# Windowed attention with sinks, then an RWKV channel mix: the first loads in one ordered queue, and q and k in rows of two tokens, cast to bf16 by GpSimd before they are transposed

## The chip, the core and the metric

The kernel runs on one core of a Trainium2 chip. The metric is the device time of one execution in microseconds (us), lower is better. Ratios use fast runs alone: runs that lie over 1.5% above the fastest of their kernel are left out of them, though the medians below still count them. The "span" is the profiled execution from its first to its last instruction; it lies 1.7 to 2.1 us below the recorded time of the same run.

## The reference, cut to what matters

Shapes: batch 4, 8 heads, 768 tokens, head size 64; model width 512, hidden width 1024; everything is fp32 in memory.

```python
# attention: each query sees the 4 first keys (sinks) and the 128 keys up to itself
keep = (pos[None, :] < 4) | ((rel >= 0) & (rel < 128))        # rel = query - key
a = softmax(where(keep, q @ k.T / 8, -1e9));  x = a @ v        # heads joined: [4, 768, 512]
# channel mix on x
xk = mu_k * x + (1 - mu_k) * x_prev;  xr = mu_r * x + (1 - mu_r) * x_prev
out = sigmoid(xr @ w_r) * (relu(xk @ w_k) ** 2 @ w_v)
```

## The kernel before

A unit is 256 tokens of one batch, so there are 12 units. Each unit has four steps, one for each pair of heads. TensorE computes scores as [key, query], ScalarE takes their exponential, VectorE multiplies with a 0/1 mask, TensorE multiplies with v (a column of ones beside v gives the sum), and VectorE normalises into `x`. TensorE then transposes `x`, ScalarE copies it to SBUF (`xt`), VectorE makes `xk` and `xr`, and the channel mix of unit u runs as small pieces (`fill()`) between the attention steps of unit u+1. TensorE's program order is fixed by the kernel; the order of the other engines is decided by the scheduler.

Scores need q and k with the head's 64 numbers on partitions, so each is transposed by TensorE. These are the parts that the change touches:

```python
def load(u):                                   # k, q, v of one unit, in rows of one token (256 bytes)
    for dst, src in ((ks, k), (qs, q), (vs, v)):
        for g in range(2):
            s0 = 256 * T + 128 * g
            nc.sync.dma_start(out=dst[:, g, :, :],
                              in_=src[b, :, s0:s0 + 128, :].rearrange("h p d -> p h d"))
...
nc.gpsimd.dma_start(out=wk_sb, in_=moe_w_k...)  # bf16 weights, cast by the transfer; wr, wv later
...
def prepare(u, part):                          # part 0, 1: k; 2, 3: q
    ps = tr_ps.tile([128, NP, 128], FP32, name="tps")
    for c in range(NP):                        # 4 fp32 transposes
        nc.tensor.transpose(out=ps[:, c, :], in_=src[:, g, 2 * c:2 * c + 2, :]..., identity=ident32)
    nc.scalar.copy(out=dst, in_=ps)            # 512 elements per partition, contiguous bf16
...
for n in range(N + 6):                         # u, c = divmod(n, 4)
    ...                                        # sink_scores(u) if c == 0; scores(n); transposes of x
    if n >= 6: fill()                          # a piece of the channel mix
    ...
    if u > 0: prepare(u + 1, c)                # one part of the next unit in every step
```

The softmax here doesn't subtract the row's maximum and nothing guards it: scores larger than these inputs give would overflow.

Of the kernel before, what the change touches and what calls it, by code (L numbers as in the profile page):

```python
# [8 lines left out]
FP32 = mybir.dt.float32  # L9
BF16 = mybir.dt.bfloat16  # L10
AX = mybir.AxisListType
AF = mybir.ActivationFunctionType
ALU = mybir.AluOpType
# [4 lines left out]
def kernel(  # L18
# [14 lines left out]
    nc = tc.nc  # L33
    B, H, S, D = q.shape
    Dm = H * D
    Dff = moe_w_k.shape[1]
    assert (B, H, S, D) == (4, 8, 768, 64) and int(window) == 128 and int(n_sink) == 4
    NS = 4
    NT = S // 256
    NP = H // 2  # L40
    NC = Dm // 128
    NF = Dff // 128
    U = B * NT
    scale = 1.0 / (D ** 0.5)

    const = ctx.enter_context(tc.tile_pool(name="const", bufs=1))
    ld = ctx.enter_context(tc.tile_pool(name="ld", bufs=3))
    kt_pool = ctx.enter_context(tc.tile_pool(name="kt", bufs=3))
# [5 lines left out]
    tr_ps = ctx.enter_context(tc.tile_pool(name="tr_ps", bufs=2, space=PSUM))  # L54
# [3 lines left out]

    raw = {}

    def load(u):
        b, T = divmod(u, NT)
        ks = ld.tile([128, 2, H, D], FP32, name="ks")
        qs = ld.tile([128, 2, H, D], FP32, name="qs")
        vs = ld.tile([128, 2, H, D], FP32, name="vs")
        for dst, src in ((ks, k), (qs, q), (vs, v)):
            for g in range(2):
                s0 = 256 * T + 128 * g
                nc.sync.dma_start(out=dst[:, g, :, :],  # L69
                                  in_=src[b, :, s0:s0 + 128, :].rearrange("h p d -> p h d"))  # L70
        raw[u] = (ks, qs, vs)

    load(0)
    load(1)


    ident32 = const.tile([128, 128], FP32, name="ident32")
    make_identity(nc, ident32)
    ident = const.tile([128, 128], BF16, name="ident")
    nc.gpsimd.tensor_copy(out=ident, in_=ident32)  # L80


    mask = const.tile([128, 2, 2, 2, 128], BF16, name="mask")
    mask0 = const.tile([128, 2, 3, 128], BF16, name="mask0")

    def keep(ap, kind):
        if kind == "U":
            nc.gpsimd.affine_select(out=ap, in_=ap, compare_op=ALU.is_ge, fill=0.0, base=-1,
                                    pattern=[[0, 2], [-1, 128]], channel_multiplier=1)
        else:  # L90
            nc.gpsimd.affine_select(out=ap, in_=ap, compare_op=ALU.is_ge, fill=0.0, base=0,
                                    pattern=[[0, 2], [1, 128]], channel_multiplier=-1)

    nc.gpsimd.memset(mask0, 1.0)
    keep(mask0[:, :, 0, :], "D")
    keep(mask0[:, :, 1, :], "U")
    keep(mask0[:, :, 2, :], "D")
    nc.gpsimd.memset(mask0[0:NS, :, 0:2, :], 1.0)

    wk_sb = const.tile([128, NC, Dff], BF16, name="wk_sb")  # L100
    wv_sb = const.tile([128, NF, Dm], BF16, name="wv_sb")
    wr_sb = const.tile([128, NC, Dm], BF16, name="wr_sb")
    wv_h = const.tile([128, NF, Dm], BF16, name="wv_h")
    nc.gpsimd.dma_start(out=wk_sb, in_=moe_w_k.rearrange("(c p) f -> p c f", p=128))
    mu_k_sb = const.tile([128, NC], FP32, name="mu_k_sb")
    nc.scalar.dma_start(out=mu_k_sb, in_=moe_mu_k.rearrange("(c p) -> p c", p=128))
    mu_r_sb = const.tile([128, NC], FP32, name="mu_r_sb")
# [7 lines left out]
    v_bufs = [const.tile([128, 2, H, D + 1], BF16, name=f"v{i}") for i in range(3)]  # L115
# [7 lines left out]
    ksink = [const.tile([128, NP * 136], BF16, name=f"ksink{i}") for i in range(2)]  # L123
# [9 lines left out]
    for t in vsink:  # L133
# [1 line left out]

    spread = const.tile([128, 128], BF16, name="spread")
    nc.gpsimd.memset(spread, 0.0)
    nc.gpsimd.tensor_copy(out=spread[0:NS, 0:4 * H].rearrange("p (h s) -> p h s", s=NS),
                          in_=ident[0:NS, 0:NS].unsqueeze(1).to_broadcast([NS, H, NS]))


    kts, qts = {}, {}

    def prepare(u, part):
        b, T = divmod(u, NT)
        ks, qs, vs = raw[u]
        g = part % 2
        if part == 0:
            kts[u] = kt_pool.tile([128, 2, NP, 128], BF16, name="kt")
            qts[u] = kt_pool.tile([128, NP, 256], BF16, name="qt")  # L150
        src, dst = ((ks, kts[u][:, g, :, :]), (qs, qts[u][:, :, 128 * g:128 * g + 128]))[part // 2]
        ps = tr_ps.tile([128, NP, 128], FP32, name="tps")
        for c in range(NP):
            nc.tensor.transpose(out=ps[:, c, :],  # L154
                                in_=src[:, g, 2 * c:2 * c + 2, :].rearrange("p a d -> p (a d)"),
                                identity=ident32)
        nc.scalar.copy(out=dst, in_=ps)  # L157
        if part < 2:
            nc.gpsimd.tensor_copy(out=v_bufs[u % 3][:, g, :, 0:D], in_=vs[:, g, :, :])  # L159
        if part == 3 and T == 0:  # L160
            kz = ksink[b % 2].rearrange("p (c w) -> p c w", w=136)
            for a in range(2):
                rows = slice(64 * a, 64 * a + 64)
                nc.gpsimd.tensor_copy(out=kz[rows, :, 4 * a:4 * a + NS],
                                      in_=kts[u][rows, 0, :, 0:NS])

    def sink_values(b):
        ps = tr_ps.tile([128, H, D], FP32, name="tps")
# [8 lines left out]
    def sink_scores(u):  # L177
        b, T = divmod(u, NT)
        ps = tr_ps.tile([128, 256], FP32, name="tps")
        for c in range(NP):  # L180
            nc.tensor.matmul(out=ps, lhsT=ksink[b % 2][:, 128 * c:128 * c + 128],  # L181
                             rhs=qts[u][:, c, :], start=(c == 0), stop=(c == NP - 1))
        es[u] = e_pool.tile([128, 256], BF16, name="es")
        nc.scalar.activation(out=es[u], in_=ps, func=AF.Exp, scale=scale)
# [19 lines left out]
    def masked(n):  # L204
        e = live[n]
        if (n // NP) % NT > 0:
            nc.vector.tensor_tensor(out=e, in0=e, in1=mask.rearrange("p a g k q -> p a (g k q)"),  # L207
                                    op=ALU.mult)
        else:
            nc.vector.tensor_tensor(out=e[:, :, 128:], in0=e[:, :, 128:],  # L210
                                    in1=mask0.rearrange("p a k q -> p a (k q)"), op=ALU.mult)
# [34 lines left out]
    def transposed(u, half):  # L246

        b, T = divmod(u, NT)
        x, xt = xs[u], xts[b % 2]
        c0 = 2 * half  # L250
        ps = tr_ps.tile([128, 2, 256], BF16, name="tps")
        for i in range(2):
            for g in range(2):
                nc.tensor.transpose(out=ps[:, i, 128 * g:128 * g + 128],  # L254
                                    in_=x[:, g, 128 * (c0 + i):128 * (c0 + i) + 128],
                                    identity=ident)
        t0 = 2 + 256 * T
        nc.scalar.copy(out=xt[:, c0:c0 + 2, t0:t0 + 256], in_=ps)
# [68 lines left out]
    N = U * NP  # L327

    def fill(count=1):
        for _ in range(count):  # L330
            next(chunks, None)

    ORDERED = {mybir.EngineType.PE}
    with tc.manual_schedule(engines=ORDERED):
        for part in range(4):
            prepare(0, part)
        for n in range(N + 6):
            u, c = divmod(n, NP)
            inner = n < N
            if inner:  # L340
                if c == 0 and u % NT > 0:
                    sink_scores(u)
                scores(n)
            if c % 2 == 1 and 2 <= n < N + 2:
                transposed((n - 2) // NP, ((n - 2) % NP) // 2)
            if n >= 6:
                fill()
            if inner:
                masked(n)
            if 1 <= n < N + 1:  # L350
                values(n - 1)
            if c % 2 == 1 and 2 <= n < N + 2:
                mix((n - 2) // NP, ((n - 2) % NP) // 2, 0)
            if n >= 6:
                fill()
            if inner and u + 1 < U:
                if u == 0 and c == 3:
                    for part in range(4):
                        prepare(1, part)
                elif u > 0:  # L360
                    prepare(u + 1, c)
                if c == 3 and u + 2 < U:
                    load(u + 2)
            if c % 2 == 0 and 3 <= n < N + 3:
                mix((n - 3) // NP, ((n - 3) % NP) // 2, 1)
            if c == 2 and inner and u % NT == 0:
                sink_values(u // NT)
            if c % 2 and n >= 6:
                fill()
            if n == 0:  # L370
                nc.gpsimd.dma_start(out=wr_sb, in_=moe_w_r.rearrange("(c p) f -> p c f", p=128))
                nc.gpsimd.dma_start(out=wv_sb, in_=moe_w_v.rearrange("(c p) f -> p c f", p=128))
            if n == 5:

                for f in range(NF):
                    nc.vector.tensor_scalar(out=wv_h[:, f, :], in0=wv_sb[:, f, :], scalar1=0.5,
                                            scalar2=None, op0=ALU.mult)
        for _ in chunks:
            pass

# [34 lines left out]
```

## Time and profile before

| | before |
|---|---|
| median | 206.14 us (4 runs, 204.73 to 208.56; 205.99 without the slow one) |
| span, mean granted TensorE clock | 203.1 us, 0.95 |
| busy: TensorE, VectorE, ScalarE, GpSimd | 178.5, 135.1, 125.3, 32.0 us |
| chain that ended last, by engine | PE 67%, DVE 11%, SPq 9%, DMA 7%, ACT 4% |
| unit 0's channel mix ends | 52.06 us |
| mean period of the next nine units | 14.15 us |

The last two rows are what the argument uses most. They are read from the instructions that write the kernel's output tile (`o_sb`, two per unit): the start of a unit's second one is taken as the end of that unit (in unit 0 that instruction itself takes 0.67 to 0.69 us in every run). The first number is the cost of the start. The difference between two units is the price of one unit once the pipeline is full. Units 0 and 9, whose distance divided by nine is the period:

```profile
52.06 0.68 DVE L315 SCALAR_TENSOR_TENSOR o_sb<-th,mm 128x512 f32<-128x512 f32 x1
179.40 0.68 DVE L315 SCALAR_TENSOR_TENSOR o_sb<-th,mm 128x512 f32<-128x512 f32 x1
```

### The profile page before, as it was taken

The numbers are of one execution on the slowest core, as the hardware profiler recorded it, in microseconds if no ns is written. First come the engines' busy times: TensorE is split into PE (matmuls) and PEld (weight loads), VectorE is DVE, ScalarE is ACT, GpSimd is POOL, SyncE is SP. The second block draws the span as 40 slices with busy tenths as digits, with TensorE's granted clock in tenths as the row PEclk, the third lists the DMA queues.
The fourth block names the chain that finished last, engine by engine and source line by source line (L and its number), as shares of the span: only waits on it lengthen the run. The fifth ranks groups of instructions, "written<-read, shape, count | busy, mean of one in ns | idle before, by whom it ended". The sixth has DMA issues, their size and how long they took to land.

```text
span 203.1 us, 4308 instructions
## 1 busy us (share of the span) xinstructions
PE 178.5 (88%) x1668; PEld 120.8 (59%) x1668; DVE 135.1 (66%) x348; ACT 125.3 (62%) x201; POOL 32.0 (16%) x68
## 2 busy tenths in 40 slices
PE   1717706899999999999999999999999999999992
PEld 1405505576765766856756767658567577566650
DVE  0026306975886977868869858868879498698731
ACT  2434604685785766876776857957767758656340
POOL 8935011313112020030030020030300000000000
PEclk9975755899999999999999999999999999999999
DMA  7999999998895995987879627402011020020202
GB/s 124 211 229 197 193 214 224 194 224 161 213 227 134 254 210 131 242 186 175 206 174 245 154 54 207 98 26 90 0 55 52 0 97 11 3 103 0 106 0 103
DMA packets 81508, 28.07 MB, mean 138 GB/s; under 512 B 76368, under 2 KB 77904, under 8 KB 81488
## 3 DMA queue, kind: packets, MB, share of 16 engines
q1 hardware_dynamic: 78336, 25.17, 57.3%
q0 software_dynamic: 2096, 2.62, 7.5%
q8 instruction: 13, 0.21, 0.4%
q10 hardware_dynamic: 1056, 0.00, 0.3%
q14 instruction: 7, 0.06, 0.1%
HBM read 24.12 MB, written 6.29 MB: 150 GB/s over the span
## 4 chain that ended last, share of the span: by engine, by line
PE 67%; DVE 11%; SPq 9%; DMA 7%; ACT 4%; issue 2%; DVEq 0%
PE mm L290 17%; PE mm L310 15%; PE mm L302 11%; SPq L69 9%; PE tps L154 7%; DMA ks<-in_k_dram 7%; PE sc L197 5%; PE o L234 4%; PE tps L254 3%; DVE o_sb L315 3%; DVE xk L277 2%; PE o L223 2%; PE tps L181 2%; ACT e L201 2%; DVE xr L277 2%
## 5 line engine op out<-in xcount | busy, mean ns | idle before, releaser
L201 ACT ACTIVATE e<-sc 128x1024 bf16<-128x1024 f32 (+1 forms) x48 | 45.9, 957 | 14.5 <-PE sc L197 12.7
L290 PE MATMUL mm<-xk,wk_sb 128*128 128x256 bf16 x384 | 50.0, 273 | 0.6 <-DVE xk L277 0.4
L310 PE MATMUL mm<-wv_h,kk 128*128 128x512 bf16 x192 | 48.3, 379 | 0.0
L207 DVE TENSOR_TENSOR e<-e,mask 128x1024 bf16<-128x1024 bf16 x32 | 22.0, 689 | 25.6 <-ACT e L201 25.5
L294 ACT ACTIVATE rl<-mm 128x512 bf16<-128x512 f32 x48 | 29.0, 603 | 15.9 <-PE mm L290 14.7
L290 PEld LDWEIGHTS <-wk_sb 128*128 128x128 bf16 x384 | 34.7, 98 | 6.2 <-issue 1.8
L159 POOL CAST v<-vs 128x512 bf16<-128x512 f32 x24 | 18.1, 767 | 112.6 <-PE o L234 53.7
L157 ACT CAST kt<-tps 128x512 bf16<-128x512 f32 x24 | 14.1, 586 | 32.0 <-PE tps L154 32.0
L154 PE MATMUL tps<-ident,ks 128*128 128x128 f32 x96 | 17.1, 311 | 12.2 <-DMA ks<-in_k_dram 12.2
L234 PE MATMUL o<-v,e 128*128 128x65 bf16 x352 | 21.3, 197 | 4.5 <-POOL v L159 4.2
L310 PEld LDWEIGHTS <-kk 128*128 128x128 bf16 x192 | 16.9, 98 | 13.1
L302 PE MATMUL mm<-wr_sb,xr 128*128 128x512 bf16 x96 | 24.4, 380 | 0.0
L234 PEld LDWEIGHTS <-e 128*128 128x128 bf16 x352 | 18.2, 100 | 8.7 <-issue 3.9
L154 PEld LDWEIGHTS tps<-ident,ks 128*128 128x128 f32 x96 | 13.5, 161 | 16.1 <-issue 7.4
L277 DVE SCALAR_TENSOR_TENSOR xr<-td,mu_r_sb,xt 128x256 bf16<-128x256 bf16 x48 | 21.7, 483 | 0.0
L295 DVE TENSOR_TENSOR kk<-rl 128x512 bf16<-128x512 bf16 x48 | 20.1, 420 | 1.9 <-ACT rl L294 1.6
L277 DVE SCALAR_TENSOR_TENSOR xk<-td,mu_k_sb,xt 128x256 bf16<-128x256 bf16 x48 | 21.2, 477 | 0.0
L210 DVE TENSOR_TENSOR e<-e,mask 128x768 bf16<-128x768 bf16 x16 | 8.9, 554 | 18.3 <-ACT e L201 17.8
L239 DVE TENSOR_TENSOR x<-o,rec 128x256 bf16<-128x256 f32 x48 | 20.1, 418 | 0.7
L197 PE MATMUL sc<-qt,kt 64*128 64x128 bf16 (+1 forms) x256 | 18.8, 248 | 1.6 <-ACT e L201 0.9
L315 DVE SCALAR_TENSOR_TENSOR o_sb<-th,mm 128x512 f32<-128x512 f32 x24 | 16.3, 679 | 3.5 <-PE mm L310 3.5
L197 PEld LDWEIGHTS <-kt 64*128 64x128 bf16 x256 | 8.9, 95 | 15.2 <-issue 14.6
(46 smaller groups left out, 168.7 us busy)
## 6 DMA issues: line engine op xcount, KB each, us to landing
ks<-in_k_dram SPq DMA_DIRECT2D x24, 256.0 KB, 4.7
qs<-in_q_dram SPq DMA_DIRECT2D x24, 256.0 KB, 4.8
vs<-in_v_dram SPq DMA_DIRECT2D x24, 256.0 KB, 5.2
out_dram<-o_sb SPq DMA_DIRECT2D x24, 256.0 KB, 2.1
wk_sb<-in_moe_w_k_dram POOLq DMA_DIRECT2D x1, 1024.0 KB, 9.5
wv_sb<-in_moe_w_v_dram POOLq DMA_DIRECT2D x1, 1024.0 KB, 12.9
wr_sb<-in_moe_w_r_dram POOLq DMA_DIRECT2D x1, 512.0 KB, 6.9
mu_k_sb<-in_moe_mu_k_dram ACTq DMA_DIRECT2D x1, 2.0 KB, 3.7
```

What stands on the lines that cost most here:

```text
L154: nc.tensor.transpose(out=ps[:, c, :], in_=src[:, g, 2 * c:2 * c + 2, :].rearrange("p a d -> p (a d)"), identity=ident32)
L197: nc.tensor.matmul(out=sc[:, a, o0:o1], lhsT=lhs[rows], rhs=qt[rows, c, q0:q0 + o1 - o0], start=True, stop=True)
L201: nc.scalar.activation(out=e[:, :, lo:], in_=sc[:, :, lo:], func=AF.Exp, scale=scale)
L207: nc.vector.tensor_tensor(out=e, in0=e, in1=mask.rearrange("p a g k q -> p a (g k q)"), op=ALU.mult)
L234: nc.tensor.matmul(out=o[:, g, a, :], lhsT=e[:, a, e0:e0 + 128], rhs=rhs, start=(T == 0 and i == 0), stop=(i == len(blocks) - 1), skip_gro ...
L239: nc.vector.tensor_tensor(out=xs[u][:, :, 128 * c:128 * c + 128].rearrange("p g (a d) -> p g a d", a=2), in0=o[:, :, :, 0:D], in1=rec.to_b ...
L277: nc.vector.scalar_tensor_tensor(out=dst[:, c0 + i, :], in0=td[:, i, :], scalar=mu[:, c0 + i:c0 + i + 1], in1=prv[:, i, :], op0=ALU.mult, ...
L290: nc.tensor.matmul(out=ps[:, i, :], lhsT=wk_sb[:, c, 128 * f:128 * f + 128], rhs=xk[:, c, :], start=(c == 0), stop=(c == NC - 1), skip_gro ...
L294: nc.scalar.activation(out=rl, in_=ps, func=AF.Relu)
L302: nc.tensor.matmul(out=ps, lhsT=xr[:, c, 128 * g:128 * g + 128], rhs=wr_sb[:, c, :], start=(c == 0), stop=(c == NC - 1))
L310: nc.tensor.matmul(out=ps, lhsT=kk[:, f, 128 * g:128 * g + 128], rhs=wv_h[:, f, :], start=(f == 0), stop=(f == NF - 1))
L315: nc.vector.scalar_tensor_tensor(out=o_sb, in0=th[g], scalar=1.0, in1=ps, op0=ALU.add, op1=ALU.mult)
```

## The change

It has four intents. All first loads go through one queue in a fixed order. q and k come in rows of two tokens (512 bytes), so partition p holds tokens 2p and 2p+1. GpSimd casts them to bf16, laid out as pairs of heads, so that their transposes are bf16 and one PSUM tile holds all of k, or q, of a unit. The pieces of the second unit's preparation move, so that channel-mix work stands ahead of the third unit's transposes. Masks, sinks and v's loads follow the new order of keys, and the weights arrive in fp32 and are cast on the engines.

```diff
-            nc.sync.dma_start(out=dst[:, g, :, :], in_=src[...].rearrange("h p d -> p h d"))
+            nc.sync.dma_start(out=t[:, hs, :, :].rearrange("p h j d -> p h (j d)"),
+                in_=src[b, hs, ...].rearrange("h (p j) d -> p h (j d)", j=2))     # k, q
 ...
+    with tc.manual_schedule(engines={SP}):
+        load(0); wk32; load(1, "kq"); wr32; load(1, "v"); wv32; load(2)           # one queue, in this order
 ...
+    def cast(u):                     # GpSimd: 2 casts each of k and q, then the 2 of v
+        halves[u, name] = kt_pool.tile([128, NP, 2, 2, D], BF16, name=name + "b")
+        nc.gpsimd.tensor_copy(out=halves[u, name][:, :, j, :, :], in_=raw[u, name][:, :, j, :]...)
 ...
-        ps = tr_ps.tile([128, NP, 128], FP32, name="tps")     # 4 fp32 transposes, 4 times a unit
+        ps = tr_ps.tile([128, NP, 2, 128], BF16, name="tps")  # 8 bf16 transposes, twice a unit
-        nc.scalar.copy(out=dst, in_=ps)
+        nc.scalar.copy(out=qts[u].rearrange("p c (t j) -> p c j t", j=2), in_=ps)
 ...
+    keep(): every mask selection in two halves of 64 partitions
+    weights_k(): 4 VectorE casts of wk, at step 2;  weights_rv(): GpSimd casts wr,
+                 VectorE scales wv to wv_h in 4 pieces, at step 4
 ...
-                elif u > 0: prepare(u + 1, c)
+                if c == 0: cast(u + 1)
+                elif c >= 2: prepare(u + 1, c - 2)            # k at step 2, q at step 3
```

## The prediction

> **What bounds the kernel now.** I read the page's table of engines and its strip of slices first, then the chain that ended last in order of time, then the timelines of single engines over the first 40 us.
>
> ```profile
> PE 178.5 (88%) x1668; PEld 120.8 (59%) x1668; DVE 135.1 (66%) x348; ACT 125.3 (62%) x201; POOL 32.0 (16%) x68
> PE   1717706899999999999999999999999999999992
> PEclk9975755899999999999999999999999999999999
> DMA  7999999998895995987879627402011020020202
> ```
>
> One digit is 5.08 us. TensorE is the bound from about slice 8 to slice 39, with two holes before that, and the DMA engines are full through exactly those early slices. The busy time of stretches says the same: in 40 to 180 us PE is busy 139.2 of 140 us. So there are two stages: a start that waits, and some 163 us in which only less TensorE work helps. The chain shows where one gives way to the other:
>
> ```profile
> 18.64 13.47 DMA ks<-in_k_dram
> 32.11 0.14 issue
> 32.25 1.09 PE tps L154 x4
> ```
>
> The columns are start, length, what. The k rows of the third unit (a unit is 256 tokens of one batch) were issued at 18.6 and landed at 32.1. The PE timeline shows what TensorE had reached by then:
>
> ```profile
> 4.41 1.09 PE L154 MATMUL tps<-ident,ks 128*128 128x128 f32 x4 [4.41 <-DMA ks<-in_k_dram]
> 14.82 0.27 PE L234 MATMUL o<-v,e 128*128 128x65 bf16 x2 [3.21 <-POOL v L159]
> 24.59 0.36 PE L234 MATMUL o<-v,e 128*128 128x65 bf16 x6
> 32.25 1.09 PE L154 MATMUL tps<-ident,ks 128*128 128x128 f32 x4 [7.29 <-DMA ks<-in_k_dram]
> ```
>
> TensorE takes its instructions in program order. Unit 0's attention is nearly done, unit 1 is prepared, but the transposes of unit 2 stand in the queue ahead of every channel-mix matmul, so 7.29 us pass idle. At 32.25 no channel mix has run at all. What is left then takes 203.1 - 32.25 = 170.85 us. That includes about 4 us of tail.
>
> What a transpose costs in the saturated stage comes from the chain and from one group:
>
> ```profile
> 39.59 0.44 PE tps L154 x4
> 187.60 0.22 PE tps L254 x4
> L154 PE MATMUL tps<-ident,ks 128*128 128x128 f32 x96 | 17.1, 311 | 12.2 <-DMA ks<-in_k_dram 12.2
> ```
>
> Four fp32 transposes of q/k hold PE's queue 0.44 us (110 ns each). Four bf16 transposes of x of the same shape hold it 0.22 us here; in the timeline at 97.78 the next matmul starts 0.25 us later (55 to 63 ns each). The 311 ns in the group are latency of pipelined instructions and not what one costs.
>
> **What the Trainium skill says, and whether this trace agrees.** "DMA: Bandwidth & Descriptors", Specifications, puts the smallest transfer at line rate at 512 bytes, and its section "Why small descriptors are slow (HBM only)" gives a 256-byte descriptor 8 beats plus about 3 cycles of overhead. The trace has the 256-byte side only: in 2.5 to 4.5 us, before the weights flow, 214 GB/s, which is 16 x 256 B / 214 GB/s = 19 ns per packet and engine. Nothing here shows 512 bytes. "TensorE: Matmul & The Clock Gate", Back-to-back issue gap, has 55.6 ns for 128 columns once warm; the 0.22 us for four agree. "ScalarE: Activation LUTs", What ACT_TABLE_LOAD costs, has 186 ns + 0.833 ns per element, so 613 ns for 512; here the copies of kt take 586 and the 1024-wide exponential 1029. "SBUF — State Buffer", SBUF: two separate sides, says GpSimd and VectorE lock each other out of a shared port pair for whole instructions. The trace fits: a GpSimd cast of v takes 0.61 us while VectorE is idle (14.15) and 0.82 at 39.10, beside which a pair of xr operations took 1.23 us where others took 0.87.
>
> **The change part by part.**
>
> *Transposes.* A unit still has 16 transposes, now bf16: 16 x 0.060 = 0.96 us for 16 x 0.110 = 1.76 us, 0.80 us saved. Units 0 and 1 are in the start, so 10 units count: 8.0 us, all on the path.
>
> *Copies out of PSUM on ScalarE.* Four of 512 (4 x 0.586 = 2.34 us per unit) become two of 1024. At 586 + 512 x 0.833 = 1013 ns each (an estimate with the skill's slope) that is 2.03. ScalarE's time is not the bound, but its latency enters: q's copy is followed at the next unit's head by the sink scores, with one channel-mix piece of 0.87 us in between. Today 0.586 us fits under 0.87; 1.01 us plus some 0.1 to 0.2 us of handover, sometimes behind a 0.6 us Relu, does not. I give this 0.2 to 0.3 us per unit, 2.5 us in all. Net of steady state: 8.0 - 2.5 = 5.5 us.
>
> *GpSimd.* It now casts k and q as well: 4 more casts of 512 elements per unit, 4 x 0.77 = 3.1 us on top of 1.5, or 4.6 in a unit of about 15 us. It keeps up. VectorE loses perhaps 0.2 us per cast by the port, 0.8 us on 11.5 us of work per unit. Still under PE.
>
> *GpSimd at the start.* This is a loss. Setup ended at 10.6 us before, and k and q did not need it; now their casts stand behind it in GpSimd's order. The build's order shows seven mask selections split in two (+7 x 0.36 = 2.5 us), one more memset (+0.47), one more small copy (+0.16), the weight issue gone (-0.88), the identity's cast gone (-0.24): setup ends near 12.6. Then two k casts with the rest of the setup between them, q's two casts done at about 16.0, v's at 17.2. Transposes of q take till 17.0, their copy till 18.1. First scores at 18.1 instead of 10.0. Before, the values then waited for v till 14.8, so 4 to 5 us are really lost.
>
> *The order of the first loads.* One queue carries k0, q0, v0, the channel mix's first matrix, k1, q1, second matrix, v1, third matrix, k2. Before k2 is complete that is 2.62 MB in 512-byte rows, 1.05 MB in 256-byte rows and 5.24 MB of fp32 weights. At 16 engines: 320 packets of 512 B at 20 to 31 ns = 6.4 to 10 us; 256 of 256 B at 19.5 = 5.0; weights at an estimated 26 GB/s per engine, 12.6 us. With a start near 3.0 (k's first 256 KB were in use at 4.4), k2 lands at 27 to 31 us, its cast ends by 32.5. So it comes 1 to 4 us earlier at most.
>
> *Pieces moved forward.* This is what I count on at the start. PE no longer meets unit 2's transposes until after four channel-mix pieces, three more score groups and two more value groups. The chain of unit 0 sets the pace: scores at 18.1, and at the present distance of 1.65 us (16.36 to 18.03) the fourth at about 22.7; exponential, mask, values, normalising and its transposes end at about 26.3; 16 transposes of unit 1 on a cold clock to 28.0; copy to 29.1; sink scores and scores to 30.2. From there TensorE has work without a gap. Between 30.2 and unit 2's transposes lie 4 x 0.87 + 3 x 0.33 + 2 x 0.36 = 5.2 us or more, so k2 is wanted at about 35 and is there.
>
> *The sum.* At 30.2 the changed kernel stands about where the old one was at 32.25: it has still unit 0's last x transposes behind it (-0.3 us of remaining work), and has done the scores that the old one had done too. So 2.0 us gained at the start, 5.5 in steady state, and 1.0 us taken off for VectorE's in-order queue, which casts the first matrix ahead of its first mask and scales the third one as soon as the queue reaches it, landed or not. Span: 203.1 - 2.0 - 5.5 + 1.0 = 196.6 us. The recorded median of 205.99 lies 2.9 above that span; the same shift gives 199.5, which I round to 199.3.
>
> **The rivals.**
>
> First, the start is lost to GpSimd. For it: GpSimd's setup is serial, 10 us long already, and everything now passes through it. Against: TensorE had 7.3 us of idle time to give away before 32.25. If GpSimd's casts run at 0.8 us and each step slips, saturation starts at 34 instead of 30.2, and the time is about 203, within 2%.
>
> Second, loads become the bound. Weights now cross as fp32 on the same queue, ahead of k2, and v in 64-partition pieces. For it: DMA is at 90% in all early slices and moves 200 GB/s whatever is asked. If the mean stayed at 205 GB/s, 8.9 MB would need 43 us; k2 would come 8 us after it is wanted: 207, the same or slower. Against: the old kernel read the same weights and 3.4 MB of rows within 30 us, about 290 GB/s of reads, and 2 to 4 KB rows have little overhead.
>
> Third, ScalarE's longer copy and the port eat the whole steady gain: 0.8 us per unit of new waiting, about 204.5. The copies' slack above makes 0.3 more likely.
>
> Fourth, better than I say: 512-byte rows as fast per packet as 256, no waits at unit heads, masks early: 8 + 5 us, about 193.
>
> **Range and chances.** The steady saving is the surest term (4 to 8 us); the start can go from -3 to +5. Adding them, 194.0 to 204.5 should hold it 8 times in 10. The 2% line is at 201.9, some 2.6 us above my figure. Faster 0.70, within 2% 0.26, slower 0.04.
>
> **What would show it.** Right: q/k transposes in the chain at 0.22 to 0.25 us per four, PE's q/k transpose work about halved; first scores near 18 us; the first channel-mix matmul near 30 us or earlier and ahead of unit 2's transposes; no wait of several us on k's loads there; POOL busy about 70 us. A wait of the sink scores on the qt copy, 0.2 to 0.3 us, about ten times. Wrong: a gap of some us before unit 2's transposes with a DMA or the k cast as releaser (the second rival); PE idle above 5 us after 40 us; masks late on VectorE because of the weight casts; PE's first saturated slice later than today's seventh or eighth.

## The result, and the profile after

The changed kernel takes 218.23 us (median of 4 runs, 216.8 to 218.66) against 206.14 us. The ratio is 1.060, with a 95% interval of 1.052 to 1.068: slower. Ratios are the mean time of one kernel's fast runs over that of the other's fast runs of the same rounds, so not quite the ratio of the medians quoted.

| | before | after |
|---|---|---|
| span, mean granted clock | 203.1, 0.95 | 216.9, 0.98 |
| busy PE, DVE, ACT, POOL | 178.5, 135.1, 125.3, 32.0 | 170.8, 152.7, 126.3, 70.9 |
| chain by engine | PE 67%, DVE 11%, ACT 4% | PE 40%, DVE 28%, ACT 16%, POOL 9% |
| unit 0 ends | 52.06 | 60.27 |
| mean period of nine units | 14.15 | 14.75 |
| last two periods | 11.21, 8.58 | 11.21, 8.58 |

The 13.8 us of span split cleanly: 8.2 at the start (60.27 - 52.06), 5.4 in the steady state (9 x 0.60), 0.2 in the tail. Units 0 and 9 after:

```profile
60.27 0.68 DVE L359 SCALAR_TENSOR_TENSOR o_sb<-th,mm 128x512 f32<-128x512 f32 x1
193.01 0.68 DVE L359 SCALAR_TENSOR_TENSOR o_sb<-th,mm 128x512 f32<-128x512 f32 x1
```

TensorE's work did fall, and both stages got longer. The page's engines and strip after, 5.42 us per digit:

```profile
PE 170.8 (79%) x1646; PEld 110.3 (51%) x1668; DVE 152.7 (70%) x348; ACT 126.3 (58%) x177; POOL 70.9 (33%) x130
PE   0004467947998788999989889989898899899992
PEclk9999999976999999999999999999999999999999
DMA  6999999900159299488496792791102011020102
```

The DMA engines now stand nearly idle in slices 8 and 9, so loads are not the bound. TensorE begins late, dips at slice 8 (43 to 49 us), has a granted clock of 0.7 and 0.6 there and in the next slice, and then stands mostly at 8 and 9 where before it stood at 9.

The chain that ended last (start, length, what) says who set the pace of the start:

```profile
17.52 1.07 POOL qb L175 x2
...
24.24 2.03 DVE e L254
...
33.84 1.21 ACT qt L200
...
41.13 2.82 DVE wv_h L386 x4
43.95 1.49 DVE kk L339 x2
```

Before, this part of the chain was one wait for a load of k. Now it runs through GpSimd's casts, then VectorE's mask, then ScalarE's copy of q, then VectorE's scaling of a weight. TensorE's timeline shows the same as its waits (start, length, then in brackets the idle time before and what ended it):

```profile
20.97 0.51 PE L241 MATMUL sc<-qt,kt 64*128 64x256 bf16 x4 [1.39 <-ACT qt L200]
26.31 0.51 PE L278 MATMUL o<-v,e 128*128 128x65 bf16 x6 [2.04 <-DVE e L254]
46.84 0.39 PE L298 MATMUL tps<-ident,x 128*128 128x128 bf16 x2 [2.88 <-DVE x L283]
```

First scores came at 20.97 (10.03 before), the first channel-mix matmul at 36.57 (36.45 before). VectorE's timeline, and two GpSimd lines beside it, give the reason for the second and third wait:

```profile
15.35 6.50 DVE L380 CAST wk_sb<-wk 128x1024 bf16<-128x1024 f32 x4 [15.35 <-DMA wk<-in_moe_w_k_dram]
24.15 2.10 DVE L254 TENSOR_TENSOR e<-e,mask 128x768 bf16<-128x768 bf16 x1
41.05 2.90 DVE L386 TENSOR_SCALAR wv_h<-wv 128x1024 bf16<-128x1024 f32 x4
```

```profile
14.52 0.61 POOL L175 CAST kb<-ks 128x512 bf16<-128x512 f32 x1
23.95 1.90 POOL L383 CAST wr_sb<-wr 128x2048 bf16<-128x2048 f32 x1
```

Unit 0's first k cast starts only at 14.52, behind GpSimd's setup. The mask multiplication that takes 0.56 us elsewhere (28.57) took 2.10 us: it started 0.20 us after GpSimd's cast of wr and ended 0.40 us after it, as if it had stood still until the cast was done. The weight casts took 1.6 us each while GpSimd cast q, k and v beside them.

In the steady state, TensorE's waits between 60 and 178 us are, before and after:

```profile
PE tps L254 <- ACT qt L157: 0.7, 3, 0.2
```

```profile
PE tps L225 <- ACT qt L200: 3.0, 5, 0.7
PE sc L241 <- ACT qt L200: 2.1, 3, 0.7
PE tps L298 <- ACT kt L191: 2.0, 3, 0.7
PE tps L298 <- DVE x L283: 1.7, 3, 1.0
PE mm L334 <- DVE xk L321: 0.7, 2, 0.5
```

(total us, times, longest.) Some eight units lie in that stretch, so 9.5 us are 1.2 us per unit where 0.1 were. Of these 5.1 are waits at a unit's head for ScalarE's copy of q. The groups by shape show the two new copies (busy, mean ns, idle before):

```profile
L200 ACT COPY qt<-tps 128x1024 bf16<-128x1024 bf16 x12 | 15.9, 1322 | 1.1 <-PE tps L197 1.1
L191 ACT COPY kt<-tps 128x1024 bf16<-128x1024 bf16 x12 | 12.1, 1009 | 14.8 <-PE tps L188 14.8
```

Same element count, but q's copy, which writes every second element, takes 1322 ns. What the change was for did happen. Eight bf16 transposes hold the queue 0.54 us (start to start), where two groups of four fp32 ones held it 0.88 us:

```profile
92.45 0.61 PE L188 MATMUL tps<-ident,kb 128*128 128x128 bf16 x8
92.99 0.40 PE L241 MATMUL sc<-qt,kt 64*128 64x256 bf16 x6
```

### The profile page after: what moved, and what is told of

The parts are those of the page before. It is cut to its first block, busy times and chain, and to the rows that moved or that the text cites. A ratio compares the mean times of both kernels' runs of the same rounds, so it can differ in the third digit from the quotient of the medians.

```text
span 216.9 us, 4338 instructions
## 1 busy us (share of the span) xinstructions
PE 170.8 (79%) x1646; PEld 110.3 (51%) x1668; DVE 152.7 (70%) x348; ACT 126.3 (58%) x177; POOL 70.9 (33%) x130
## 4 chain that ended last, share of the span: by engine, by line
PE 40%; DVE 28%; ACT 16%; POOL 9%; issue 6%; POOLq 0%; ACTq 0%; DVEq 0%
PE mm L334 12%; PE mm L354 9%; PE mm L346 6%; ACT qt L200 5%; DVE xk L321 5%; DVE o_sb L359 4%; ACT e L245 4%; PE sc L241 4%; ACT rl L338 3%; PE o L278 3%; DVE xr L321 3%; DVE e L254 3%; DVE kk L339 3%; DVE e L251 3%; DVE x L283 3%
## 5 line engine op out<-in xcount | busy, mean ns | idle before, releaser
L334 PE MATMUL mm<-xk,wk_sb 128*128 128x256 bf16 x384 | 51.8, 276 | 1.3 <-DVE xk L321 0.7
L354 PE MATMUL mm<-wv_h,kk 128*128 128x512 bf16 x182 | 45.3, 379 | 0.5
L251 DVE TENSOR_TENSOR e<-e,mask 128x1024 bf16<-128x1024 bf16 x32 | 23.4, 731 | 29.9 <-ACT e L245 29.9
L175 POOL CAST kb<-ks 128x512 bf16<-128x512 f32 x24 | 17.1, 739 | 28.1 <-DMA ks<-in_k_dram 27.9
L321 DVE SCALAR_TENSOR_TENSOR xr<-td,mu_r_sb,xt 128x256 bf16<-128x256 bf16 x48 | 24.9, 538 | 0.0
L339 DVE TENSOR_TENSOR kk<-rl 128x512 bf16<-128x512 bf16 x48 | 21.9, 458 | 2.3 <-ACT rl L338 2.3
L321 DVE SCALAR_TENSOR_TENSOR xk<-td,mu_k_sb,xt 128x256 bf16<-128x256 bf16 x48 | 22.0, 489 | 0.0
L175 POOL CAST qb<-qs 128x512 bf16<-128x512 f32 x24 | 17.1, 743 | 14.3 <-DMA qs<-in_q_dram 13.3
L188 PE MATMUL tps<-ident,kb 128*128 128x128 bf16 x96 | 8.4, 234 | 16.5 <-POOL kb L175 16.5
L191 ACT COPY kt<-tps 128x1024 bf16<-128x1024 bf16 x12 | 12.1, 1009 | 14.8 <-PE tps L188 14.8
```

The source lines that it names most:

```text
L175: nc.gpsimd.tensor_copy(out=halves[u, name][:, :, j, :, :], in_=raw[u, name][:, :, j, :].rearrange("p (c a) d -> p c a d", a=2))
L251: nc.vector.tensor_tensor(out=e, in0=e, in1=mask.rearrange("p a g k q -> p a (g k q)"), op=ALU.mult)
L321: nc.vector.scalar_tensor_tensor(out=dst[:, c0 + i, :], in0=td[:, i, :], scalar=mu[:, c0 + i:c0 + i + 1], in1=prv[:, i, :], op0=ALU.mult, ...
L334: nc.tensor.matmul(out=ps[:, i, :], lhsT=wk_sb[:, c, 128 * f:128 * f + 128], rhs=xk[:, c, :], start=(c == 0), stop=(c == NC - 1), skip_gro ...
L339: nc.vector.tensor_tensor(out=kk[:, 2 * f2:2 * f2 + 2, :], in0=rl, in1=rl, op=ALU.mult)
L354: nc.tensor.matmul(out=ps, lhsT=kk[:, f, 128 * g:128 * g + 128], rhs=wv_h[:, f, :], start=(f == 0), stop=(f == NF - 1))
```

## The experiments

Twelve kernels ran; all were correct within the reference's tolerance. "Unit 0 ends" and "period" (mean of nine) are read as above.

| run | built on | median us | ratio to before (95%) | unit 0 ends | period |
|---|---|---|---|---|---|
| before | | 205.0 to 206.1 | 1 | 52.06 | 14.15 |
| after | | 218.23 | 1.060 (1.052 to 1.068) | 60.27 | 14.75 |
| e1_q_early | after | 211.58 | 1.028 (1.024 to 1.032) | 55.43 | 14.41 |
| e2_no_casts | after | 211.20 | 1.028 (1.025 to 1.032) | 56.94 | 14.33 |
| e3_masks_first | after | 213.32 | 1.040 (1.035 to 1.045) | 57.62 | 14.45 |
| e4_casts_first | after | 212.86 | 1.037 (1.033 to 1.042) | 55.15 | 14.64 |
| e5_q_early_no_casts | after | 205.14 | 1.000 (0.996 to 1.005) | 54.17 | 13.93 |
| e6_order_only | before | 205.79 | 1.003 (0.999 to 1.007) | 53.61 | 14.12 |
| e7_start | after | 207.17 | 1.009 (1.005 to 1.014) | 49.28 | 14.72 |
| e8_start_q_early | e7 | 207.10 | 1.007 (0.999 to 1.014) | 50.92 | 14.63 |
| e9_dma_cast | e7 | 200.93 | 0.978 (0.973 to 0.982) | 49.23 | 14.05 |
| e10_act_k | e7 | 203.12 | 0.992 (0.985 to 0.998) | 48.77 | 14.25 |
| e11_flat_copy | after | 224.67 | 1.096 (1.091 to 1.100) | 61.06 | 15.27 |
| e12_q_natural | e9 | 198.77 | 0.969 (0.965 to 0.972) | 48.45 | 13.80 |

The theory: the start is lost to serial work on GpSimd and VectorE, and the steady state to two separate things, the latency of q's copy at the unit's head and VectorE slowed by GpSimd's casts. Rivals: the loads and the new order of pieces; TensorE or ScalarE itself.

### e1_q_early: the transposes of k and q one step earlier

```diff
-                elif c >= 2: prepare(u + 1, c - 2)
+                elif c <= 2: prepare(u + 1, c - 1)          # k at step 1, q at step 2
```

> Edit: the k and q transposes of the next unit move one step earlier (steps 1 and 2 of a unit instead of 2 and 3), so that the qt copy (1.32 us) has a whole step to land before the sink scores. Theory A (in steady state TensorE loses its time at unit heads, waiting for that copy; the changed kernel has 6.4 us of sink scores waiting for qt and 3.5 us of scores waiting for qt, 7 us of it after 50 us): these waits vanish, the period of a unit falls from 14.75 us to about 14.1, time about 212 us. Theory B (VectorE, slowed by GpSimd's casts, sets the pace): the waits move to the xk and x operands and the time stays above 216.5 us.

The period fell from 14.75 to 14.41. The waits of a unit's head on q's copy are gone from the stretch 60 to 178 us (5.1 us after the change). In exchange the wait of x's transposes on `x` rose to 6.1 us there (1.7), and 2.8 us of the same transposes wait behind q's copy:

```profile
PE tps L298 <- DVE x L283: 6.1, 5, 2.2
PE tps L298 <- ACT qt L200: 2.8, 3, 0.9
```

So the latency of the copy at the head was real, and worth 0.34 us per unit, about half of what was expected. Moving it exposes VectorE. Unit 0 ended 4.8 us earlier too, although the first channel-mix matmul stood at 36.61 as before it: the idle time behind the scaling of wv was 2.15 us instead of 2.88, and the strip of the granted clock has no digit below 9.

### e2_no_casts: from unit 2 on, GpSimd casts neither k nor q

This kernel is wrong: units 2 and up use the q and k of units 0 and 1. It passes the tolerance only because the scores of these inputs are tiny.

```diff
         for name in "kq":
+            if u >= 2:
+                halves[u, name] = halves[u % 2, name]; continue
```

> Wrong result on purpose: from unit 2 on the k and q casts on GpSimd are left out and the transposes read the casts of units 0 and 1 again; everything else stays. Theory B (port contention of the casts with VectorE): xr falls from 538 to about 485 ns, the 768-wide mask from 718 to about 555, VectorE's busy time from 152.7 to about 143 us, the period from 14.75 to about 14.2 us and the time to about 212 us. Theory A (the qt copy's latency): the waits on qt stay near 8 us and the time stays within 2 us of the changed kernel's (above 216).

The period fell to 14.33, although the waits on q's copy stayed (3.1 + 2.1 us in the same stretch). Where the gain came from is seen in VectorE's groups between 70 and 160 us, first of the changed kernel, then of this one:

```profile
L321 DVE SCALAR_TENSOR_TENSOR xr<-td,mu_r_sb,xt 128x256 bf16<-128x256 bf16 x25 | 13.8, 569 | 0.0
L251 DVE TENSOR_TENSOR e<-e,mask 128x1024 bf16<-128x1024 bf16 x16 | 12.1, 756 | 14.4 <-ACT e L245 14.4
```

```profile
L324 DVE SCALAR_TENSOR_TENSOR xr<-td,mu_r_sb,xt 128x256 bf16<-128x256 bf16 x26 | 11.8, 472 | 0.0
L254 DVE TENSOR_TENSOR e<-e,mask 128x1024 bf16<-128x1024 bf16 x16 | 11.0, 689 | 16.2 <-ACT e L248 16.2
```

Without the casts the same operations are back at the durations of the kernel before (477 and 690 ns in this stretch). GpSimd's casts cost VectorE 97 ns on each xr and 67 on each mask, and the kernel 0.42 us per unit. Here too the idle time behind the scaling of wv was shorter (1.30 us) and the clock did not fall afterwards, and unit 0 ended 3.3 us earlier. What the low clock of the changed kernel cost can be read off: the same TensorE work, from the end of this wait to the start of the next, took 5.31 us there (46.84 to 52.15) and 2.81 us here (45.97 to 48.78), so 2.5 us. The lines that bound these stretches (46.84 is shown above), first of the changed kernel, then of this one:

```profile
53.53 0.60 PE L225 MATMUL tps<-qt,ksink 128*128 128x256 bf16 x4 [1.38 <-ACT qt L200]
```

```profile
45.97 0.29 PE L301 MATMUL tps<-ident,x 128*128 128x128 bf16 x2 [1.30 <-DVE x L286]
50.21 0.60 PE L228 MATMUL tps<-qt,ksink 128*128 128x256 bf16 x4 [1.43 <-ACT qt L203]
```

### e3_masks_first and e4_casts_first: the start, one engine at a time

e3 makes VectorE issue the first masks in program order, with the weight casts behind them. e4 makes GpSimd cast unit 0's q, k and v right after the small mask, ahead of the rest of its setup.

```diff
 e3: +        head.enter_context(tc.manual_schedule(engines={DVE}))       # until step 3
     -            if n == 2: weights_k()
     +            if n == 3: weights_k(); head.close()
 e4: +    setup.enter_context(tc.manual_schedule(engines={Pool}))
      memset(...small mask...)
     +    cast_qk(0, "k"); ones of v_bufs; cast_qk(0, "q"); cast_v(0)     # was: after all of the setup
```

> Edit: VectorE issues unit 0's masks and normalisations before the four casts of the first matrix, which stood first in its queue (6.5 us from 15.35, so that the first mask ran only at 22.43). If these casts hold the start up: unit 0's values come about 2 us earlier, the first channel-mix matmul at about 34.5 instead of 36.6 us, time about 216 us. If GpSimd's chain (casts behind setup) sets the start alone: first mask at 22.4 as before, no change (218). The casts may also land on the path further on, ahead of the last normalisation of unit 0: then 218 to 220.

> Edit: GpSimd's order at the start is fixed: identity, first mask, then unit 0's casts of k, q and v, then the rest of the setup. If the casts' place behind the setup is what delays the start: the first scores come at about 12 us instead of 21, the first channel-mix matmul at about 30 instead of 36.6, time 212 to 214 us, with a wait before unit 2's transposes for k2 (landed at about 32.5). If the loads set the start: first channel-mix matmul after 35 us and time above 217. VectorE's first mask behind the first matrix's casts (15.4 to 21.9) could eat most of the gain: then first values at about 22.5 and time about 217.

Each gained only part: unit 0 ended at 57.62 and 55.15 instead of 60.27. In e4 the first scores came at 11.10, ten us earlier, and yet the first channel-mix matmul came at 36.42 where it was 36.57. TensorE waited 5.14 us for GpSimd's sink setup, now pushed back, and 4.18 us for an `x` whose VectorE was casting weights. In e3 the first channel-mix matmul came even later (38.20), and TensorE waited 3.73 us for `x` behind the weight casts. The theory that these casts hold up the first mask was a miss: in the changed kernel they end at 21.85 and the first exponential only at 22.32. The wait of 3.73 us cannot be compared with the one that comes before the low clock in the changed kernel. It lies before TensorE has reached full pace: eight channel-mix matmuls of e3 take 1.89 us at first and 1.04 from 40.93 on.

```profile
38.20 1.89 PE L334 MATMUL mm<-xk,wk_sb 128*128 128x256 bf16 x8
40.93 1.04 PE L334 MATMUL mm<-xk,wk_sb 128*128 128x256 bf16 x8
```

(The strip of the clock shows 9 in those first slices too, so there neither it nor the mean clock says anything about the pace.) After full pace was reached, the profiles of variants of the change show a fall in e11 (behind a wait of 2.89 us) and twice in e8 (waits of 2.63 and 2.21 us), and none in e1 behind 2.15 us. No run tells what length of idleness brings it. VectorE's and GpSimd's lines of e3 settle what slows a VectorE operation:

```profile
22.86 1.82 DVE L254 TENSOR_TENSOR e<-e,mask 128x768 bf16<-128x768 bf16 x1 [0.65 <-ACT e L245]
29.82 2.49 DVE L380 CAST wk_sb<-wk 128x1024 bf16<-128x1024 f32 x4
```

```profile
22.37 1.90 POOL L383 CAST wr_sb<-wr 128x2048 bf16<-128x2048 f32 x1 [0.57 <-DMA wr<-in_moe_w_r_dram]
```

With nothing beside them (GpSimd waited for a load from 26 to 33 us) the four weight casts took 2.49 us instead of 6.50. The mask that met GpSimd's cast of wr again ended 0.4 us after that cast (24.68 against 24.27). It is the company, not the operation, that is slow.

### e5_q_early_no_casts: both steady causes removed

This is e1 and e2 together, wrong as e2 is.

> Wrong result on purpose: q's transposes a step earlier and no k/q casts from unit 2 on, both edits at once. If the qt copy's latency and the port contention are the two causes that ate the steady gain, the period falls to 13.4 to 13.7 us (14.15 of the kernel before less the 0.8 us of cheaper transposes is 13.35), waits of TensorE on qt and x nearly vanish, time about 204 us. If the two only add what they gave one by one (0.34 and 0.42 us), the period is 14.0 and the time about 207. If something else holds the pace, the period stays at 14.3 and the time above 209.

The period is 13.93, 0.82 us below the changed kernel's; e1 and e2 alone gave 0.34 and 0.42. The causes add, and they explain more than the 0.60 us by which the changed kernel's period exceeded the old one. The rest of the expected gain does not appear: 2.8 us of waits behind q's copy and 2.5 us on `x` remain in the stretch.

### e6_order_only: the kernel before with the new queue and order alone

Old rows, old fp32 transposes, old masks; the ordered queue, fp32 weights cast on the engines, and the new order of pieces.

> The kernel before with only the one ordered queue of loads (fp32 weights on it, cast by VectorE and GpSimd as in the change) and the changed order of pieces on TensorE; rows of 256 bytes, fp32 transposes straight from the loads and no q/k casts stay as they were. If GpSimd's casts of q and k are what made the change slow, this is not slower than the kernel before: period about 14.15, time 200 to 206 us. If the new queue or the new order of pieces is to blame: above 210 us, with the loss in the first 60 us.

It is as fast as before (ratio 1.003), with the old period. Channel-mix matmuls started at 26.75 instead of 36.45, and then TensorE waited 7.04 us for the third unit's k, until 34.84:

```profile
26.75 1.05 PE L295 MATMUL mm<-xk,wk_sb 128*128 128x256 bf16 x8
34.84 1.09 PE L159 MATMUL tps<-ident,ks 128*128 128x128 f32 x4 [7.04 <-DMA ks<-in_k_dram]
```

So the queue and the order neither cost nor gain; they moved the old hole. In the changed kernel, k of the third unit had landed at 32.5, ten us before TensorE wanted it. The rival of the loads falls.

### e7_start and e8_start_q_early: the start repaired on all engines together

```diff
 e7: GpSimd in program order: small mask, unit 0's casts, sinks, unit 1's k and q casts, large mask last
     VectorE and ScalarE in program order through step 4
-            if n == 2: weights_k()
+            (at step 4, behind unit 0's last normalisation) weights_k()
-        nc.gpsimd.tensor_copy(out=wr_sb, in_=wr32)
+        nc.scalar.copy(out=wr_sb, in_=wr32)
 e8: e7 with the earlier transposes of e1
```

> The start repaired, steady state as in the change: GpSimd casts k, q, v of unit 0 right after the first mask, then sets up the sinks, casts unit 1's k and q and only then builds the large mask; VectorE casts the first matrix behind unit 0's last normalisation; ScalarE casts the second matrix. If these orders are the whole loss of the start: end of unit 0's channel mix at 51 to 53 us instead of 60.3, no idle of TensorE over 3 us after 30 us, time about 209 to 211. If the loads bound the start anyway (k2 landed near 32.5): end of unit 0 at 54 or later and time above 212.

> The start of the run before together with q's transposes a step earlier. If start and steady state are separate losses: about 6 us less than that run, 203 to 205 us, level with the kernel before. If VectorE's contention takes the place of the qt wait: period 14.4 and about 207.

e7's first channel-mix matmul is at 27.78 and unit 0 ends at 49.28, 11 us earlier than in the changed kernel and 2.8 earlier than before. The period stayed at 14.72, as it should: the two losses are separate. Several orders change at once in e7, and beyond e3 and e4 no run tells what each is worth. The time, 207.17, is better than the 209 to 211 expected. e8 came out at 207.10 where 203 to 205 was hoped for. The transposes of unit 2 then came too early and waited 2.63 and 0.73 us for GpSimd's casts, so unit 0 ended at 50.92. The granted clock of this profile also fell twice, in slices 6 and 7 and again in 20, counted from 0 (5.17 us a slice; this run was the slowest of e8's four, 205.75 to 208.39):

```profile
PEclk9999998599999999999979999999999999999998
```

The period came out at 14.63, with 6.3 us of waits on `x`. One unit of 16.18 us, which holds the second fall, makes much of that; the other eight average 14.44, as in e1 (14.41). So the gain of e1 is there in the steady state, and e8 spends it on the start and on the clock.

### e9_dma_cast and e10_act_k: the q/k casts taken off GpSimd

Both have e7's start, and the earlier transposes from unit 3 on only (e8's lesson; the recorded text says unit 2). e9 also keeps GpSimd in program order through the whole loop, which e10 does not; no run separates this from the cast in the transfer.

```diff
 e9:  +            if name != "v" and u >= 3:          # bf16 head pairs straight from the transfer
      +                t = halves[u, name] = kt_pool.tile([128, 2, H, D], BF16, name=name + "d")
      +                for j in range(2):
      +                    nc.gpsimd.dma_start(out=t[:, j], in_=src[...].rearrange("h (p j) d -> j p h d", j=2)[j])
 e10: -            nc.gpsimd.tensor_copy(
      +            (nc.scalar.copy if u >= 3 and name == "k" else nc.gpsimd.tensor_copy)(
```

> An attempt to beat both kernels: the repaired start of e7_start, q/k transposes one step earlier for units 2 to 11 (as in e1_q_early), and from unit 3 on k and q are cast to bf16 by the transfer itself, so GpSimd's engine does no q/k cast in the loop. Theory (the steady loss is the copy's latency at the unit's head plus VectorE slowed beside GpSimd's casts): the additions of e5_q_early_no_casts come without its wrong results. VectorE's xr near 472 and mask near 690 ns again, period at most 13.95 us, unit 0 ends near 49.5, so time 197 to 201, faster than before. Rival A (the cast in the transfer costs more than it saves: rows of 128 bytes written, descriptors made by GpSimd): PE waits on the bf16 rows or on v casts queued behind the issues, period 14.5 or more, time 205 to 212. Rival B (what the period still lacks is TensorE's own work and x waits, which no cast changes): period 14.2, time about 202.

> As e9_dma_cast in start and order, but the k casts of units 3 and up go to ScalarE and q's stay on GpSimd. Theory of the shared port: VectorE's slowing is about halved against e8 (xr near 505, mask near 710 ns), period about 14.2, time about 203. Rival (ScalarE is already the second chain: exponential, Relu and copies): two more copies of some 0.6 us per unit make the exponentials late, PE waits on ScalarE rise by over 0.4 us per unit, period 14.6 or more, time 207 or more.

e9 took 200.93 us, within what was expected, and beats the kernel before by 2.2%; whether by the 2% that counts as faster here is unclear (interval 1.8 to 2.7%). Its period of 14.05 misses the 13.95 expected (over units 2 to 8 it is 13.98, against 14.66 after the change). Masks of 1024 are at 691 ns between 70 and 160 us, but xr only fell to 505, not 472. The reason is v's casts, still on GpSimd: two of the 26 xr started while one ran and took 829 and 832 ns, the others about 478. Issuing a transfer holds GpSimd 0.9 us, as long as a cast, so its busy time did not fall (78.3 us in all). VectorE's operations were nevertheless faster. e10 at 203.12 lies between, as the theory had it: xr 503 ns, period 14.25, and ScalarE, though 9 us busier, did not become the bound.

### e11_flat_copy: is the stride the reason for q's long copy?

```diff
-            nc.scalar.copy(out=qts[u].rearrange("p c (t j) -> p c j t", j=2), in_=ps)
+            nc.scalar.copy(out=qts[u], in_=ps.rearrange("p c j t -> p c (j t)"))
-                                 rhs=qt[rows, c, q0:q0 + o1 - o0], ...
+                                 rhs=qt[rows, c].rearrange("p (j t) -> p t j", j=2)[:, q0 // 2:..., :], ...
```

> The changed kernel with one thing undone: ScalarE copies q's transposes flat (contiguous), and the interleave of the two tokens of a row is made by TensorE's strided read of q in the scores and sink scores. Theory (the strided 2-byte write is what makes this copy 1322 instead of 1009 ns, and PE waits 6.4 + 3.5 us on it): copy near 1010 ns, waits on it fall by about 0.3 us per unit to 5 to 6 us in sum, time 213.5 to 216, if a strided read costs TensorE nothing. Rival A: the length is not from the stride but from what runs beside it; copy stays near 1.3, time 218. Rival B: the strided read slows the score matmuls (12 x 256 columns per unit and the sinks'), PE's score time rises by over 10% and the time does not fall.

The answer is yes, and the rival that the stride only moves is right too. The copy fell to 1008 ns, and the time rose by 6 us, because TensorE's score matmuls now read with a stride:

```profile
L200 ACT COPY qt<-tps 128x1024 bf16<-128x1024 bf16 x12 | 12.1, 1008 | 1.1 <-PE tps L197 1.1
L242 PE MATMUL sc<-qt,kt 64*128 64x256 bf16 x96 | 19.9, 410 | 3.1 <-ACT qt L200 1.9 <-ACT e L248 1.2
```

The same 96 matmuls took 292 ns in the changed kernel. On the engine that is the bound, 118 ns a matmul is dearer than 314 ns a copy on the engine that is not.

### e12_q_natural: no stride anywhere

e9, with q from unit 3 on in plain token order. Only k and v must agree in their order; q need not follow it.

```diff
-                            "h (p j) d -> j p h d", j=2)[j])
+                            "h (p j) d -> j p h d" if name == "k" else "h (j p) d -> j p h d", j=2)[j])
+            if u >= 3: nc.scalar.copy(out=qts[u], in_=ps.rearrange("p c j t -> p c (j t)"))
```

> e9_dma_cast with one change: from unit 3 on q is loaded in plain token order (token 128 g + p on partition p), so that ScalarE's copy of q's transposes is contiguous; TensorE's reads stay contiguous too, unlike in e11_flat_copy. Theory (the strided 2-byte write costs 0.3 us on the path of the unit's head or delays the exponentials behind it): the copy takes about 1010 ns instead of 1300 in units 3 to 11, period 13.6 to 13.8 instead of 13.87, ratio to before 0.965 to 0.977. Rival (with the transposes one step earlier the copy is hidden and ScalarE has slack): the copy shrinks all the same, period 13.87, ratio 0.977 to 0.98 as in e9_dma_cast.

The period fell to 13.80 and the time to 198.77 us, 3.1% below the kernel before and outside e9's interval. The copy and what is left of TensorE's waits between 60 and 178 us:

```profile
L236 ACT COPY qt<-tps 128x1024 bf16<-128x1024 bf16 x9 | 9.1, 1006 | 0.0
```

```profile
PE tps L336 <- ACT qt L236: 1.9, 3, 0.7
PE tps L336 <- DVE x L321: 1.6, 3, 0.7
```

These 3.5 us are 0.4 us per unit, after 1.2 in the changed kernel. Against that kernel, e12 gains 11.8 us at the start (60.27 - 48.45) and 9 x 0.944 = 8.5 in nine periods, together 20.3 of the 20.4 us between the spans (216.9 and 196.5). What did not settle: why e12's period is still 13.8 and not the 13.47 that the saved transposes alone would give (14.15 less the measured 0.68; 13.35 with the predicted 0.80). Waits of 0.4 us per unit are listed; no run tells whether they could be had.

## Why the prediction was wrong

The prediction was 199.3 us and faster; the kernel takes 218.23 us. Its own account was -2.0 at the start, +1.0 for VectorE's queue, -5.5 in the steady state. Measured: +8.2, and +5.4. Two slips come on top, neither of them decisive. The shift of 2.9 us from span to time set the median beside the span of another run (the profiled run took 204.83, so 1.7). The fourth score group at 18.1 + 3 x 1.65 is 23.05, not 22.7.

**Transposes (right, a little small).** Predicted 0.80 us per unit saved. Measured 4 x 0.44 - 2 x 0.54 = 0.68 us. The mechanism is as told.

**Copies on ScalarE (the mechanism right, the term too small).** The step put q's copy at 1.01 us and the wait at 0.2 to 0.3 us per unit. k's copy is 1.009 us, as estimated; q's is 1.322, because it writes with a stride, which the estimate left out although the diff shows it (e11: 1.008 without). The wait at the head was 5.1 us in eight units, 0.64 each, with another 0.25 each where x's transposes wait behind k's copy. This is 0.89 us in place of 0.25: the third rival's 0.8 us per unit was the right size, and the prediction called it less likely.

**GpSimd's casts beside VectorE (the step that failed in kind).** The prediction saw the contention, put it at 0.8 us of VectorE's time per unit, and dismissed it because VectorE is "still under PE". VectorE's busy time per unit rose by some 1.0 us (69.3 of 90 us at a period of 14.15, 72.7 of 90 at 14.75). But a busy share is no slack: the masks, `xk` and `xr` and the squares are links of a chain that TensorE meets several times per unit, and they got longer (between 70 and 160 us xr from 477 to 569 ns, masks from 690 to 756, squares from 413 to 448; `x` itself stayed at 416 to 419). e2 shows what it cost, 0.42 us per unit.

Together TensorE idles 1.3 us more per unit (busy 89.5 of 90 us before, 81.6 after, each scaled to its period), less 0.68 saved: 0.6 us more, which is the change of the period.

**GpSimd at the start (right in kind, too small).** Setup was to end at 12.6; it ended at 14.5. The main part is the mask selections. The step charged 0.36 us for each of seven more; the fourteen halves took 0.45 us each from start to start, so 14 x 0.45 - 7 x 0.36 = 3.8 us instead of 2.5. First scores were at 20.97 instead of 18.1.

**"The chain of unit 0 sets the pace" (failed).** The step led from first scores at 18.1 to work without a gap at 30.2, in 12.1 us. Measured were 20.97 to 36.57 for the first channel-mix matmul, 15.6 us. Of the 6.4 us by which this point came late, 2.9 lie before the first scores, 1.6 between the first and the fourth scores (27.18), 0.95 up to unit 1's transposes (31.73 instead of 26.3), and 0.94 in these and their copies. One cause is seen directly, the wait of 2.04 us for a mask that stood beside GpSimd's cast of wr. The waits for `x` (2.00 in two) and for q's copy (1.45) do not come from the weight casts alone: e7, where wr's cast is on ScalarE and wk's stand behind the last normalisation, has 2.37 and 1.46 us of the same. It needs 16.4 us from first scores to first channel-mix matmul (11.38 to 27.78), 1.89 of them for the sink setup. Why this chain is longer than predicted stays open beyond the mask.

Then a hole that no step had: at 41.05 VectorE scaled wv for 2.90 us ahead of the squares and masks, TensorE idled 2.88 us, and the granted clock fell to 0.7 and 0.6 in two slices of 5.42 us, which cost another 2.5 us by the comparison under e2. The whole allowance for VectorE's queue was 1.0 us. e7 confirms the start as a whole: its first scores come 9.6 us earlier, its longest wait between 30 us and that end is 1.51 us, its clock does not fall, and unit 0 ends 11 us earlier, 2.8 us ahead of the kernel before. That is the gain that the prediction wanted.

**The loads (right in kind, 1.5 us late).** k of the third unit landed at 32.5, later than the 27 to 31 predicted, and was wanted only at 42.8. The sum gave the weights 12.6 us; at the 391 to 408 GB/s that they moved in three stretches of the run, 5.24 MB take 12.8 to 13.4 us, an estimate. The second rival fell, and the piece order by itself is neutral (e6).

**Range and chances.** The start was allowed -3 to +5 and came at +8.2; the steady saving was called the surest term and had the wrong sign. Both errors come from one habit: a cost on an engine with spare busy time was counted as nothing. The signs named as "wrong" were the ones that came: idle TensorE after 40 us, masks late on VectorE because of the weight casts, and a later first saturated slice.

## What to carry to other kernels

When work moves to an engine that has time to spare, ask where it stands in that engine's order at the start, and whom it locks out while it runs; a busy share answers neither. A GpSimd cast can cost VectorE nearly its own length where the two meet (1.5 us of a 1.9 us cast here), so a cast that the transfer can do, or another engine can, is worth more than its own duration. A layout that saves one engine work should be followed to every later reader and writer: here one tensor (q) did not need the new token order at all, and leaving it out removed a strided copy at no cost.

## What the Trainium skill lacked or had wrong

- "SBUF — State Buffer", SBUF: two separate sides, says that the engine that starts first gets the shared pair for the whole instruction and the other fully blocks. The runs agree, and the numbers are worth having there: a mask of 0.56 us took 2.10 and 1.82 us, each time ending 0.4 us after a GpSimd cast of 1.90 us; four fp32 to bf16 casts took 2.49 us alone and 6.50 us beside GpSimd work that was mostly casts. Issuing a casting transfer from GpSimd, 0.9 us of its time, left masks at 691 ns in the mean, as before the change (690), though one beside two such issues and no cast took 777 (e9).
- "SBUF — State Buffer", Door 1: The DMA port swizzle, says that accesses which stay within a 16-byte line run at full bandwidth and those that cross to a new line pay a penalty, without figures. ScalarE's write of every second bf16 element stays within its line and still took 1322 ns where the contiguous write took 1009. TensorE's read of q in steps of 256 bytes, which does cross, took 410 ns for a 64x256 score matmul instead of 292.
- "DMA: Bandwidth & Descriptors", Specifications, gives 512 bytes as the smallest transfer at line rate. The 512-byte rows of the first loads moved 294 to 298 GB/s in three stretches, where the weights' 2 to 4 KB rows moved 391 to 408 GB/s. 256-byte rows moved 210 to 218 before the change, with short stretches at 279 and 286.
- No page has the cost of a GpSimd mask selection: 256 elements took 402 ns on 64 partitions and 410 to 417 on 128, so splitting one by partitions doubles it.
